# Top 32 of 576 scores on VectorE: the largest of each four keys, with three candidate sets of eight, in place of the larger of each two keys with one set

## The chip, the cores and the metric

The kernel runs on one core of one Trainium2 chip. The core has five engines with a queue each: TensorE (PE in the profile, PEld its weight loads), VectorE (DVE), ScalarE (ACT), GpSimd (POOL) and SyncE (SP), which here only issues DMA transfers. The metric is the device time of one run in microseconds (us); lower is better.

## The reference

Attention with a top 32 of each row of scores, then a layer norm and a two-layer MLP with a residual:

```python
q, k, v: (8, 8, 576, 64)                       # batch, heads, rows, head width
scores = scale * np.matmul(q, k.transpose(0, 1, 3, 2))
kth = np.partition(scores, -32, axis=-1)[..., -32:-31]
scores = np.where(scores >= kth, scores, -1e9)
scores = scores - scores.max(axis=-1, keepdims=True)
attn = np.exp(scores)
attn = attn / (attn.sum(axis=-1, keepdims=True) + 1e-09)
x = matmul(attn, v) with the heads side by side   # (8, 576, 512)
xn = (x - mean) / sqrt(var + 1e-06) * g_ln
out = x + relu(xn @ w_ch1) @ w_ch2               # 512 -> 2048 -> 512
```

## The kernel before

**Units and steps.** The scores are made in units. A full unit is 128 query rows of two heads: two tiles, each 128 rows x 576 scores. A rest unit takes the last 64 rows of two heads as one tile of 128 x 576. There are 128 full and 32 rest units. The main loop (from L1263) makes one step for each unit, and the order of all instructions is written out in it by hand. In step n, VectorE selects on unit n in four stretches (`select(u, 0)` to `select(u, 3)`, L1309, L1342, L1377, L1396) and then prepares the next unit (`halve(nxt)`, L1398). In the same step ScalarE and GpSimd make the mask of unit n-1 (`prepare`, `mask`, L1291 to L1293), PE makes the scores of unit n+2, and the unit before those is transposed and multiplied by V. Between these pieces calls of `fill()` put matmuls of the MLP, as many as a planner has given to the step; its costs (`DVE_UNIT`, L1175) are constants that do not depend on what is measured.

**Finding the threshold.** VectorE has an instruction that gives the eight largest of a row (MAX8) and one that overwrites these eight in the row (MATCH_REPLACE8, with a value load before it). The 32nd largest needs four rounds. Before the change a row of 576 is folded once: `halve` (L447) writes the larger of each pair (j, j+288) to `hi` (L461) and the smaller to `lo` (L462). Rounds 0 and 1 work on the 288 larger ones alone. Eight candidates from `lo` (L475) are put beside `hi`, and rounds 2 and 3 work on 296. `hi` lives in one of two home buffers; the place of the candidates in it changes sides every second unit, so that they can still be read when the next unit of that home is written.

**The mask.** When the last MAX8 (L483) of unit n is done, ScalarE scales the threshold and the maximum (L495, L496) and for each tile writes a step function of the scores (L532); GpSimd subtracts the scores from it (L535); ScalarE takes the exponential (L543).

**The watch.** If eight of a row's top 32 lay in `lo`, eight candidates would not be known to be enough. So GpSimd notes for each row and tile the last candidate less the threshold (L502, two numbers for a full unit). Every 16 units VectorE reduces the notes (L512), and at the end one number (`tell`, L517) says whether the whole program is to be run again with 16 candidates (L1444).

The pool `lo` has one buffer for each tag (L70).

Of the kernel before, what the change touches and what calls it, by code (L numbers as in the profile page):

```python
# [10 lines left out]
ALU = mybir.AluOpType  # L11
FP32 = mybir.dt.float32
# [17 lines left out]
def compute(  # L30
# [12 lines left out]
    nc = tc.nc  # L43
# [15 lines left out]

    NV = 2  # L60
    GQ = 2 * P + R
    HALF = S // 2
    LOWS = 8 * low_rounds

    consts = pool("consts", 1)
    ldpool = pool("ld", 1)
# [24 lines left out]
    def const(shape, name):  # L91
        return consts.tile(shape, FP32, tag=name, name=name)
# [12 lines left out]
    ends = const([P, P], "ends")  # L105
    nc.gpsimd.memset(ends[:], 0.0)
    if doubt is not None:
        watched = const([P, 2, 34], "watched")
        nc.gpsimd.memset(watched[:], -1.0)
    hi_homes = [const([P, 2, HALF + (1 if doubt is None else 2) * LOWS], f"hi{i}") for i in range(2)]  # L110
    ident = const([P, P], "ident")
    make_identity(nc, ident[:])
    columns = const([P, J + NC], "columns")
# [333 lines left out]
    def halve(u):  # L447

        nt = len(u.tiles)
        u.lo = lopool.tile([P, 2, HALF], FP32, tag="lo", name="lo")
        u.hi = hi_homes[u.i % 2]
        sides = int(doubt is not None)
        u.low, u.body = (sides * LOWS + HALF, sides * LOWS) if doubt is None or u.i // 2 % 2 else (0, LOWS)
        a, b = u.sc[:, 0:nt, 0:HALF], u.sc[:, 0:nt, HALF:S]
        lo, hi = u.lo[:, 0:nt], u.hi[:, 0:nt, u.body : u.body + HALF]  # L460
        nc.vector.tensor_tensor(hi, a, b, ALU.max)  # L461
        nc.vector.tensor_tensor(lo, a, b, ALU.min)  # L462

    def select(u, i):

        nt = range(len(u.tiles))

        def replace(m, t, x):
            nc.vector.match_replace(x, m[:, t, :], x, LOWEST)  # L469

        if i == 1:
            for r in range(low_rounds):
                o = u.low + 8 * r
                for t in nt:
                    nc.vector.max(u.hi[:, t, o : o + 8], u.lo[:, t])  # L475
                if r < low_rounds - 1:
                    for t in nt:
                        replace(u.hi[:, :, o : o + 8], t, u.lo[:, t])
        r0, width = (min(u.low, u.body), HALF + LOWS) if i > 1 else (u.body, HALF)
        pl = brief_small if i in (1, 2) else small  # L480
        m = pl.tile([P, 2, 8], FP32, tag=f"m{i}", name=f"m{i}")
        for t in nt:
            nc.vector.max(m[:, t, :], u.hi[:, t, r0 : r0 + width])  # L483
        if i < TOP_K // 8 - 1:
            for t in nt:
                replace(m, t, u.hi[:, t, r0 : r0 + width])
        if i == 0:
            u.top = m
        u.thr = m
# [8 lines left out]
    def watch(u):  # L498

        nt = len(u.tiles)  # L500
        half, c = u.i // 16 % 2, 1 + 2 * (u.i % 16)
        nc.gpsimd.tensor_tensor(  # L502
            watched[:, half, c : c + nt], u.hi[:, 0:nt, u.low + 7], u.thr[:, 0:nt, 7], ALU.subtract
        )
        if u.i % 16 == 15 or u.i == N - 1:
            u.ends_watch = True
            u.half = half

    def settle_watch(half):

        for out, first, op in ((0, 0, ALU.max), (33, 1, ALU.min)):
            nc.vector.tensor_reduce(  # L512
                watched[:, half, out : out + 1], watched[:, half, first : first + 33],
                mybir.AxisListType.X, op,
            )

    def tell():  # L517

        w = hpool.tile([P, J * P], FP32, tag="h", name="tell")
        nc.gpsimd.memset(w[:], 0.0)  # L520
        nc.vector.tensor_scalar(w[:, 2:4], watched[:, :, 33], -1.0e38, None, ALU.is_le)
        nc.vector.tensor_scalar(w[:, 4:6], watched[:, :, 0], 0.0, None, ALU.is_ge)
        nc.vector.tensor_reduce(w[:, 0:1], w[:, 2:6], mybir.AxisListType.X, ALU.max)
        ps = brief("tell")
# [952 lines left out]
```

## Time and profile before

| | |
|---|---|
| Median of 3 runs | 1571.16 us (1571.02 to 1571.75) |
| The profiled execution's own time | 1571.11 us |
| Its span (first to last instruction) | 1569.2 us |
| Mean granted TensorE clock | 0.975 |

The page of the profile has the busy time of each engine, the span in 40 slices, the DMA queues, the chain of work that ended last and the costliest groups of instructions. Further views answer questions: busy time by stages of the span, instructions in order of time, a table of who waited for whom, groups kept apart by shape. Names like `hi<-sc` give the tile written and the tile read; L461 is line 461 of the kernel. Busy time of PE is modelled, so a busy PE is not PE at its peak. The profile is of one execution, and the sums made from it are compared with that execution's own time.

### The profile page before, as it was taken

How to read it: one execution, taken by the hardware profiler on the slowest of the kernel's cores; microseconds unless marked ns; L12 is line 12 of the kernel's file. 1: busy time of each engine (PE TensorE's matmuls, PEld its weight loads, DVE VectorE, ACT ScalarE, POOL GpSimd, SP SyncE). 2: the span in 40 equal slices, each digit the busy share in tenths (PEclk: the TensorE clock that was granted, in tenths of full speed). 3: DMA queues.
4: the chain of work that ended last, by engine and by line, in shares of the span. 5: the costliest groups of instructions: out<-in, count | busy, mean ns of one | idle time of the engine just before them, and what ended most of it. 6: DMA issues, size and time to landing. Idle time of an engine off the chain costs nothing. (4 is left out here: it accounts for less than half of the span.)

```text
span 1569.2 us, 27215 instructions
## 1 busy us (share of the span) xinstructions
PE 1469.0 (94%) x8046; PEld 1108.0 (71%) x8046; DVE 1363.4 (87%) x3873; ACT 1083.8 (69%) x3081; POOL 981.2 (63%) x1318
## 2 busy tenths in 40 slices
PE   4568889999999999999999999999999998999997
PEld 3346446566787677778777777777777776788886
DVE  7997999899979998999988999999999999768000
ACT  6978887786777767767768676768676776555421
POOL 6968995747465565756566647474746475737524
PEclk9779989999999999999999999999999999999999
DMA  6623551466728865577754687657677557454511
GB/s 170 167 85 97 137 139 53 124 178 181 226 83 194 202 208 153 168 199 153 216 148 134 174 200 197 173 150 191 175 201 206 162 164 208 121 166 125 150 35 50
DMA packets 374774, 245.60 MB, mean 157 GB/s; under 512 B 255956, under 2 KB 343512, under 8 KB 374616
## 3 DMA queue, kind: packets, MB, share of 16 engines
q1 hardware_dynamic: 371048, 243.17, 57.6%
q8 instruction: 67, 1.10, 0.3%
q10 hardware_dynamic: 3568, 0.59, 0.3%
q14 instruction: 91, 0.75, 0.2%
HBM read 166.14 MB, written 77.53 MB: 155 GB/s over the span
## 5 line engine op out<-in xcount | busy, mean ns | idle before, releaser
L535 POOL TENSOR_TENSOR e<-e,sc 128x576 f32<-128x576 f32 x288 | 416.0, 1462 | 453.8 <-ACT e L532 392.9
L819 PE MATMUL hps<-xT,w 128*128 128x256 f32 x2304 | 542.2, 384 | 2.4 <-ACT xT L781 2.4
L819 PEld LDWEIGHTS hps<-xT,w 128*128 128x128 f32 x2304 | 423.0, 191 | 82.2 <-issue 27.2
L483 DVE MAX8 m<-hi 128x8 f32<-128x296 f32 (+1 forms) x1152 | 471.3, 444 | 1.2
L469 DVE MATCH_REPLACE8 hi<-m,hi 128x288 f32<-128x288 f32 (+1 forms) x864 | 377.0, 441 | 0.0
L979 PE MATMUL ops<-w,h 128*128 128x256 f32 x1280 | 304.8, 383 | 1.4 <-ACT o L944 1.4
L979 PEld LDWEIGHTS ops<-w,h 128*128 128x128 f32 x1280 | 233.6, 190 | 44.3 <-issue 13.5
L419 ACT COPY sc<-scps 128x288 f32<-128x288 f32 x576 | 188.5, 402 | 78.5 <-POOL e L535 56.2
L543 ACT ACTIVATE e<-e,m 128x576 f32<-128x576 f32 x288 | 225.1, 784 | 14.6 <-POOL e L535 12.5
L532 ACT ACTIVATE e<-sc,m 128x576 f32<-128x576 f32 x288 | 209.4, 769 | 0.0
L842 ACT ACTIVATE h<-hps 128x512 f32<-128x512 f32 x144 | 86.7, 602 | 114.1 <-PE hps L819 113.5
L577 DVE STREAM_TRANSPOSE sc<-e 128x1152 f32<-128x1152 f32 x87 | 118.8, 1366 | 52.5 <-ACT e L543 46.3
L669 PE MATMUL av<-pt,vb 128*64 128x256 f32 (+2 forms) x1280 | 148.8, 376 | 9.5 <-DMA pt<-turned 7.7
L462 DVE TENSOR_TENSOR lo<-sc 128x576 f32<-128x576 f32 (+1 forms) x160 | 136.1, 850 | 0.0
L461 DVE TENSOR_TENSOR hi<-sc 128x576 f32<-128x576 f32 (+1 forms) x160 | 130.0, 812 | 3.0 <-ACT sc L419 3.0
L669 PEld LDWEIGHTS av<-pt,vb 128*64 128x64 f32 x1280 | 81.6, 140 | 66.4 <-issue 17.1
L438 PE MATMUL scps<-kT,late_qT 64*128 64x288 f32 (+3 forms) x832 | 121.7, 410 | 0.2 <-ACT pt L618 0.2
L979 PE MATMUL ops<-wt,s 128*128 128x256 f32 x512 | 119.4, 383 | 0.0
L475 DVE MAX8 hi<-lo 128x8 f32<-128x288 f32 x288 | 117.5, 443 | 0.0
L438 PE MATMUL scps<-kT,qT 64*128 64x288 f32 x512 | 92.6, 460 | 23.5 <-DVE qT L366 8.0
L606 PE MATMUL tp<-ident,e 128*128 128x128 f32 x456 | 74.2, 290 | 39.9 <-ACT e L543 28.9
L979 PEld LDWEIGHTS ops<-wt,s 128*128 128x128 f32 x512 | 94.7, 190 | 17.3 <-issue 4.4
(111 smaller groups left out, 1793.5 us busy)
## 6 DMA issues: line engine op xcount, KB each, us to landing
turned<-sc SPq DMA_DIRECT2D x87, 576.0 KB, 4.2
pt<-turned SPq DMA_DIRECT2D x348, 144.0 KB, 3.2
w<-forms SPq DMA_DIRECT2D x128, 256.0 KB, 4.7
vb<-in_v_dram SPq DMA_DIRECT2D x80, 288.0 KB, 4.2
raw<-in_moe_w_ch_dram SPq DMA_DIRECT2D x32, 512.0 KB, 4.5
kT<-kept SPq DMA_DIRECT2D x48, 288.0 KB, 3.7
kept<-kT SPq DMA_DIRECT2D x32, 288.0 KB, 3.6
kqin<-in_k_dram SPq DMA_DIRECT2D x116, 72.0 KB, 2.6
```

What stands on the lines that cost most here:

```text
L419: nc.scalar.copy(u.sc[:, t, s * HALF : (s + 1) * HALF], u.made[s][t][:, 0:HALF])
L438: nc.tensor.matmul(ps[i * R : i * R + ql, o : o + width], qT[r, q0 : q0 + ql], kT[r, k0 : k0 + width], start=True, stop=True,)
L461: nc.vector.tensor_tensor(hi, a, b, ALU.max)
L462: nc.vector.tensor_tensor(lo, a, b, ALU.min)
L469: nc.vector.match_replace(x, m[:, t, :], x, LOWEST)
L483: nc.vector.max(m[:, t, :], u.hi[:, t, r0 : r0 + width])
L532: nc.scalar.activation(u.e[:, t], u.sc[:, t], AF.Relu, bias=u.edge[:, t : t + 1], scale=-STEEP)
L535: nc.gpsimd.tensor_tensor(u.e[:, t], u.e[:, t], u.sc[:, t], ALU.subtract)
L543: nc.scalar.activation(u.e[:, t], u.e[:, t], AF.Exp, bias=u.bias[:, t : t + 1], scale=-scale, accum_out=g.den[:, col : col + 1],)
L669: nc.tensor.matmul(av[h * D : (h + 1) * D, 0 : g.nq], vb[:, h * (J + 1) + c, :], heads_of(g, h, 0, g.nq // 32)[:, :, c], start=(c == 0), s ...
L819: nc.tensor.matmul(ps[0][:, side * N : (side + 1) * N], w1[:, c, f * P : (f + 1) * P], self.xT[:, c, 0:N], start=(c == 0), stop=(c == NC - 1),
L979: nc.tensor.matmul(bank[name][:, 0:Q], a(j), rhs, start=first and j == 0, stop=(j == G - 1), skip_group_check=not first,)
```

## The change

The row of 576 is folded twice. `halve` writes the larger of each pair to a tile `pairs` of 288 and folds that again: the larger ones, the largest of each four keys (144), go to `hi`, and the smaller ones, the seconds of this fold (144), to a new tile `mid`. The smaller halves of the first fold go to `lo` as before; `pairs` and `lo` share a tag, so they share one buffer. In `select`, round 0 works on the 144; after it eight candidates are taken from each half of `mid` (72 each), and in the second stretch eight from `lo`, as before; rounds 1 to 3 work on 168, the 144 and 24 candidates. The watch notes the last candidate of each of the three sets, so the notes are three times as many. The second pass (`doubt is None`) keeps the single fold. The planner's constants are not touched.

```diff
--- before.py
+++ after.py
@@ -59,8 +59,10 @@
 
     NV = 2
     GQ = 2 * P + R
-    HALF = S // 2
+    HALF, QUART = S // 2, S // 4
     LOWS = 8 * low_rounds
+    POOLS = 3
+    CANDS = 8 * POOLS
 
     consts = pool("consts", 1)
     ldpool = pool("ld", 1)
@@ -105,9 +107,11 @@
     ends = const([P, P], "ends")
     nc.gpsimd.memset(ends[:], 0.0)
     if doubt is not None:
-        watched = const([P, 2, 34], "watched")
+        NOTES = POOLS * 32
+        watched = const([P, 2, NOTES + 2], "watched")
         nc.gpsimd.memset(watched[:], -1.0)
-    hi_homes = [const([P, 2, HALF + (1 if doubt is None else 2) * LOWS], f"hi{i}") for i in range(2)]
+    home = HALF + LOWS if doubt is None else QUART + 2 * CANDS
+    hi_homes = [const([P, 2, home], f"hi{i}") for i in range(2)]
     ident = const([P, P], "ident")
     make_identity(nc, ident[:])
     columns = const([P, J + NC], "columns")
@@ -452,14 +456,25 @@
 
 
         nt = len(u.tiles)
+        u.hi = hi_homes[u.i % 2]
+        a, b = u.sc[:, 0:nt, 0:HALF], u.sc[:, 0:nt, HALF:S]
+        tt = nc.vector.tensor_tensor
+        if doubt is None:
+            u.lo = lopool.tile([P, 2, HALF], FP32, tag="lo", name="lo")
+            u.low, u.body, u.width = HALF, 0, HALF
+            tt(u.hi[:, 0:nt, 0:HALF], a, b, ALU.max)
+            tt(u.lo[:, 0:nt], a, b, ALU.min)
+            return
+        u.low, u.body = (CANDS + QUART, CANDS) if u.i // 2 % 2 else (0, CANDS)
+        u.width = QUART
+        pairs = lopool.tile([P, 2, HALF], FP32, tag="lo", name="pairs")
+        tt(pairs[:, 0:nt], a, b, ALU.max)
+        x, y = pairs[:, 0:nt, 0:QUART], pairs[:, 0:nt, QUART:HALF]
+        u.mid = lopool.tile([P, 2, QUART], FP32, tag="mid", name="mid")
+        tt(u.hi[:, 0:nt, u.body : u.body + QUART], x, y, ALU.max)
+        tt(u.mid[:, 0:nt], x, y, ALU.min)
         u.lo = lopool.tile([P, 2, HALF], FP32, tag="lo", name="lo")
-        u.hi = hi_homes[u.i % 2]
-        sides = int(doubt is not None)
-        u.low, u.body = (sides * LOWS + HALF, sides * LOWS) if doubt is None or u.i // 2 % 2 else (0, LOWS)
-        a, b = u.sc[:, 0:nt, 0:HALF], u.sc[:, 0:nt, HALF:S]
-        lo, hi = u.lo[:, 0:nt], u.hi[:, 0:nt, u.body : u.body + HALF]
-        nc.vector.tensor_tensor(hi, a, b, ALU.max)
-        nc.vector.tensor_tensor(lo, a, b, ALU.min)
+        tt(u.lo[:, 0:nt], a, b, ALU.min)
 
     def select(u, i):
 
@@ -468,15 +483,24 @@
         def replace(m, t, x):
             nc.vector.match_replace(x, m[:, t, :], x, LOWEST)
 
-        if i == 1:
-            for r in range(low_rounds):
-                o = u.low + 8 * r
+        if doubt is None:
+            if i == 1:
+                for r in range(low_rounds):
+                    o = u.low + 8 * r
+                    for t in nt:
+                        nc.vector.max(u.hi[:, t, o : o + 8], u.lo[:, t])
+                    if r < low_rounds - 1:
+                        for t in nt:
+                            replace(u.hi[:, :, o : o + 8], t, u.lo[:, t])
+            with_all, cands = i > 1, LOWS
+        else:
+            if i == 1:
                 for t in nt:
-                    nc.vector.max(u.hi[:, t, o : o + 8], u.lo[:, t])
-                if r < low_rounds - 1:
-                    for t in nt:
-                        replace(u.hi[:, :, o : o + 8], t, u.lo[:, t])
-        r0, width = (min(u.low, u.body), HALF + LOWS) if i > 1 else (u.body, HALF)
+                    nc.vector.max(u.hi[:, t, u.low : u.low + 8], u.lo[:, t])
+            with_all, cands = i > 0, CANDS
+        r0, width = u.body, u.width
+        if with_all:
+            r0, width = min(u.low, u.body), width + cands
         pl = brief_small if i in (1, 2) else small
         m = pl.tile([P, 2, 8], FP32, tag=f"m{i}", name=f"m{i}")
         for t in nt:
@@ -484,6 +508,14 @@
         if i < TOP_K // 8 - 1:
             for t in nt:
                 replace(m, t, u.hi[:, t, r0 : r0 + width])
+        if i == 0 and doubt is not None:
+            part = QUART // (POOLS - 1)
+            for t in nt:
+                for r in range(POOLS - 1):
+                    o = u.low + 8 + 8 * r
+                    nc.vector.max(
+                        u.hi[:, t, o : o + 8], u.mid[:, t, r * part : (r + 1) * part]
+                    )
         if i == 0:
             u.top = m
         u.thr = m
@@ -498,9 +530,13 @@
     def watch(u):
 
         nt = len(u.tiles)
-        half, c = u.i // 16 % 2, 1 + 2 * (u.i % 16)
+        half, c = u.i // 16 % 2, 1 + 2 * POOLS * (u.i % 16)
+        cands = u.hi[:, 0:nt, u.low : u.low + CANDS].rearrange("p t (r k) -> p t r k", k=8)
         nc.gpsimd.tensor_tensor(
-            watched[:, half, c : c + nt], u.hi[:, 0:nt, u.low + 7], u.thr[:, 0:nt, 7], ALU.subtract
+            watched[:, half, c : c + POOLS * nt].rearrange("p (t r) -> p t r", r=POOLS),
+            cands[:, :, :, 7],
+            u.thr[:, 0:nt, 7].unsqueeze(2).to_broadcast([P, nt, POOLS]),
+            ALU.subtract,
         )
         if u.i % 16 == 15 or u.i == N - 1:
             u.ends_watch = True
@@ -508,9 +544,9 @@
 
     def settle_watch(half):
 
-        for out, first, op in ((0, 0, ALU.max), (33, 1, ALU.min)):
+        for out, first, op in ((0, 0, ALU.max), (NOTES + 1, 1, ALU.min)):
             nc.vector.tensor_reduce(
-                watched[:, half, out : out + 1], watched[:, half, first : first + 33],
+                watched[:, half, out : out + 1], watched[:, half, first : first + NOTES + 1],
                 mybir.AxisListType.X, op,
             )
 
@@ -518,7 +554,7 @@
 
         w = hpool.tile([P, J * P], FP32, tag="h", name="tell")
         nc.gpsimd.memset(w[:], 0.0)
-        nc.vector.tensor_scalar(w[:, 2:4], watched[:, :, 33], -1.0e38, None, ALU.is_le)
+        nc.vector.tensor_scalar(w[:, 2:4], watched[:, :, NOTES + 1], -1.0e38, None, ALU.is_le)
         nc.vector.tensor_scalar(w[:, 4:6], watched[:, :, 0], 0.0, None, ALU.is_ge)
         nc.vector.tensor_reduce(w[:, 0:1], w[:, 2:6], mybir.AxisListType.X, ALU.max)
         ps = brief("tell")
```

## The prediction

> **What bounds the kernel now.** I read the page's busy shares first.
> ```profile
> span 1569.2 us, 27215 instructions
> ...
> PE 1469.0 (94%) x8046; PEld 1108.0 (71%) x8046; DVE 1363.4 (87%) x3873; ACT 1083.8 (69%) x3081; POOL 981.2 (63%) x1318
> ```
> TensorE (PE) looks like the bound, but these are averages. So I asked for the busy time by stages (columns: length, then busy us and instruction count of PE, its weight loads, VectorE (DVE), ScalarE (ACT), GpSimd (POOL), then clock and DMA).
> ```profile
> 480.00:600.00 120.00, 114.02 (x647) 87.38 (x646) 119.55 (x345) 85.38 (x250) 66.47 (x92) 0.99 0.78 201
> 600.00:720.00 120.00, 118.95 (x760) 92.67 (x760) 110.68 (x319) 88.54 (x272) 73.81 (x109) 1.00 0.63 164
> ...
> 840.00:960.00 120.00, 117.31 (x648) 88.69 (x647) 119.48 (x344) 86.28 (x249) 74.15 (x110) 1.00 0.74 188
> 960.00:1080.00 120.00, 118.73 (x663) 90.24 (x663) 119.38 (x347) 87.81 (x260) 72.75 (x107) 1.00 0.61 165
> 1080.00:1200.00 120.00, 118.96 (x644) 89.85 (x642) 119.25 (x340) 87.19 (x253) 72.56 (x111) 1.00 0.71 190
> 1200.00:1320.00 120.00, 115.46 (x630) 86.56 (x627) 119.45 (x349) 84.46 (x251) 74.62 (x109) 1.00 0.63 179
> ...
> 1480.00:1569.00 89.00, 79.17 (x383) 68.08 (x381) 1.64 (x4) 17.72 (x42) 32.76 (x63) 0.96 0.19 55
> ```
> From 480 to 600 and from 840 to 1320 us VectorE is busy 119.2 to 119.6 of each 120 us: nothing can be put in there without making the step longer. PE does more matmuls in a stage where VectorE has gaps (760 against 630 to 663), so in the saturated stages it is not at its limit, but it is near it. The last 89 us belong to PE alone. Then the table of waits (waiter <- what it waited for: us, times, longest):
> ```profile
> POOL e L535 <- ACT e L532: 392.9, 111, 10.2
> ...
> ACT m L495 <- DVE m L483: 84.2, 51, 3.7
> ACT sc L419 <- POOL e L535: 56.2, 25, 4.4
> DVE sc L577 <- ACT e L543: 46.3, 10, 9.3
> ...
> ACT e L543 <- POOL e L535: 12.5, 20, 1.7
> ```
> In 51 of the 160 unit steps ScalarE stands idle until VectorE's last MAX8 of the unit (L483) has come: there it starts on the mask at once. Keep this 51.
>
> **One unit's work on VectorE, from the timeline.** A step in a saturated stage (columns: start us, length us, what):
> ```profile
> 1232.49 0.74 DVE L461 TENSOR_TENSOR hi<-sc 128x576 f32<-128x576 f32 x1
> ...
> 1232.84 1.44 ACT L532 ACTIVATE e<-sc,m 128x576 f32<-128x576 f32 x2
> ...
> 1233.14 0.75 DVE L462 TENSOR_TENSOR lo<-sc 128x576 f32<-128x576 f32 x1
> ...
> 1233.69 2.85 POOL L535 TENSOR_TENSOR e<-e,sc 128x576 f32<-128x576 f32 x2 [3.98 <-ACT e L532]
> ...
> 1233.81 0.81 DVE L483 MAX8 m<-hi 128x8 f32<-128x288 f32 x2
> ...
> 1234.54 0.07 DVE L469 MATCH_VALUE_LOAD hi<-m,hi 128x8 f32 x1
> 1234.60 0.44 DVE L469 MATCH_REPLACE8 hi<-m,hi 128x288 f32<-128x288 f32 x1
> ...
> 1234.96 0.08 DVE L469 MATCH_VALUE_LOAD hi<-m,hi 128x8 f32 x1
> ...
> 1235.39 0.81 DVE L475 MAX8 hi<-lo 128x8 f32<-128x288 f32 x2
> ...
> 1236.12 0.80 DVE L483 MAX8 m<-hi 128x8 f32<-128x288 f32 x2
> ...
> 1237.68 0.83 DVE L483 MAX8 m<-hi 128x8 f32<-128x296 f32 x2
> 1238.43 0.07 DVE L469 MATCH_VALUE_LOAD hi<-m,hi 128x8 f32 x1
> ...
> 1240.03 0.44 DVE L461 TENSOR_TENSOR hi<-sc 128x288 f32<-128x288 f32 x1
> 1240.39 0.45 DVE L462 TENSOR_TENSOR lo<-sc 128x288 f32<-128x288 f32 x1
> 1240.76 0.45 DVE L483 MAX8 m<-hi 128x8 f32<-128x288 f32 x1
> 1241.25 0.09 DVE L469 MATCH_VALUE_LOAD hi<-m,hi 128x8 f32 x1
> ```
> What counts is the distance from one start to the next, which I call the slot, not the length, because the end of one instruction overlaps the start of the next. A TENSOR_TENSOR over 576 elements has a slot of 0.65 to 0.67 us (1232.49 to 1233.14 to 1233.81), over 288 one of 0.36; a MAX8 over 288 has 0.365 (two in 0.73), a MATCH_REPLACE8 0.36 (1234.60 to 1234.96), its value load 0.065. So a slot is 0.06 us plus 1.04 ns an element, which is (0.66-0.36)/288. An instruction that needs the result of the one just before it comes later: 1240.76 to 1241.25 is 0.49 where 0.365 is the slot, 0.12 more. The step runs 7.54 us (1232.49 to 1240.03) without a gap.
>
> **The change, part by part.** A full unit (two tiles; 128 of them) has 8 MAX8 and 6 MATCH_REPLACE8 on 288 or 296 elements, and 2 MAX8 on the smaller halves. Without its two TENSOR_TENSOR that is 7.54 - 1.32 = 6.22 us.
>
> MAX and replace: afterwards slots by the formula are 0.21 (144 elements), 0.235 (168) and 0.135 (72). Two MAX8 on 144 and six on 168 make 1.83; two on the smaller halves stay 0.73; four new ones on 72 make 0.54; two replaces on 144 and four on 168 make 1.36; six value loads 0.40. Sum 4.86, which is 1.36 us less. (With the four TENSOR_TENSORs below, a full unit issues 30 instructions, where it had 24.) With two tiles in turn no dependent pair stands back to back, so no 0.12 is added.
>
> The TENSOR_TENSORs: two become four. The pair maxima over 576 cost 0.66, and the next one reads them, so 0.78 until it starts; the fours' maxima 0.36; the fours' seconds 0.36, and then the smaller halves are written into the buffer that the seconds are read from, so that instruction waits for them too: 0.48; then 0.67. Sum 2.29 against 1.32: 0.97 more. Undisturbed, a full unit gains 1.36 - 0.97 = 0.39 us. A rest unit (one tile; 32 of them) has its MAX and replace in a dependent row; by the same slots it saves 0.56 and pays 0.66: 0.10 us more.
>
> Now the collision, which decides. These rows show a TENSOR_TENSOR pair on VectorE into which the mask's subtraction on GpSimd falls:
> ```profile
> 710.50 0.74 DVE L461 TENSOR_TENSOR hi<-sc 128x576 f32<-128x576 f32 x1
> 710.78 1.73 POOL L535 TENSOR_TENSOR e<-e,sc 128x576 f32<-128x576 f32 x1 [6.76 <-ACT e L532]
> ...
> 711.15 1.97 DVE L462 TENSOR_TENSOR lo<-sc 128x576 f32<-128x576 f32 x1
> ...
> 713.05 0.81 DVE L483 MAX8 m<-hi 128x8 f32<-128x288 f32 x2
> ```
> ```profile
> L535 POOL TENSOR_TENSOR e<-e,sc x288: 1394/1413/2648, 30.3 to 1465.4; 128x576 f32<-128x576 f32 x144
> ```
> ```profile
> L461 DVE TENSOR_TENSOR hi<-sc x160: 429/737/1978, 11.3 to 1440.8; 128x576 f32<-128x576 f32 x128, 128x288 f32<-128x288 f32 x32
> ```
> ```profile
> L462 DVE TENSOR_TENSOR lo<-sc 128x576 f32<-128x576 f32 x128 | 117.6, 918 | 0.0
> ...
> L461 DVE TENSOR_TENSOR hi<-sc 128x576 f32<-128x576 f32 x128 | 114.5, 895 | 3.0 <-ACT sc L419 3.0
> ```
> GpSimd's instruction started 0.28 us into VectorE's first one, took 1.73 instead of its median 1.41, so it was held for 0.32, until VectorE's first had read for 0.60; then VectorE's second one, due at 711.15, took 1.97 instead of 0.75, 1.22 more. The two engines take turns, one whole instruction each, in the order in which they ask, and MAX8 and MATCH_REPLACE8 take no part (in the quiet step above they keep their 0.44 while GpSimd's two run from 1233.69 to 1236.54). In the quiet step above the subtraction comes 1.20 us after the first TENSOR_TENSOR (1233.69 - 1232.49): in the last one, so VectorE loses nothing and GpSimd 0.07. ScalarE's way to the mask starts at the end of the unit's last MAX8 and the change leaves it as it is, so the subtraction will again ask at 1.20. But then VectorE is at the third of four (it starts at 0.78 + 0.36 = 1.14 and reads until 1.44) and the fourth is due at 1.62. GpSimd gets in at 1.44, holds until 2.85, and the fourth runs from 2.85, 1.23 us late. What is queued behind it is the next unit's whole selection, and all of PE's and ScalarE's work that hangs on it. Such a unit costs -0.39 + 1.23 = 0.84 us more than before. The second subtraction then waits for the fourth's 0.60 us of reading and ends 4.86 us after the first TENSOR_TENSOR instead of 4.05 (1.20 + 2.85); ScalarE's exponentials (L543) wait for it, and ScalarE has some 30 us idle in each 120.
>
> [...]
>
> Small things: the watch on GpSimd subtracts six numbers instead of two, four elements more in the 4 us for which GpSimd waits for ScalarE anyway (3.98 in the row above); if that cover were gone it would be some ns each. The 20 reductions of the notes read 97 instead of 33 elements, 64 x 1.04 ns x 20 = 1.3 us. The wait for the watch of the unit four before moves from the second stretch of the selection to the first, some 2 us earlier; that watch is over two steps old by then. PE, ScalarE and SyncE issue the same instructions in the same order, DMAs included.
>
> **The sum.** 128 full units undisturbed: -0.39 x 128 = -50. 32 rest units: +3. The subtraction that asks at 1.20: 51 steps by the row of waits, x 1.23 = +63. Other collisions (weight conversion, sums of the MLP): L461 and L462 now stand at 895 and 918 ns, and undisturbed at 740 and 750, so they cost (155 + 168) x 128 = 41 us; with four instructions to be cut into instead of two, what comes on top lies between 0 and 41. The reading time goes up by half (0.60 + 0.30 + 0.30 + 0.60 = 1.80 against 1.20), which would be 20 more; the number of entries doubles, which would be 41; I take 30. Notes +1. Sum +47. Some falls into the stages in which VectorE has idle time (9.3 of 120 us at 600 to 720) and from 1480 us on VectorE has almost nothing to do: I keep +45 on the profiled run's own time of 1571.1 us (span 1569.2 and 1.9 around it; the median of the runs is 1571.16, the same): **1616 us**. The ends: nothing of the last 30 and 30 collisions instead of 51 give 47 - 30 - 26 = -9, so 1562; collisions in 70 steps and the full 41 of the others give 47 + 23 + 11 = +81, so 1652.
>
> **Rivals.**
> (a) The subtraction misses the cluster, because ScalarE is late or VectorE goes first: then the 0.39 is gained, in the saturated stages only, since PE is near its limit. 600 us of such stages are some 75 steps of about 8 us (7.54, or 8.9 with a transpose in it), 128/160 of them full: 60 x 0.39 = 23, so 1548. For it: only 51 of 160 steps are of the prompt kind. Against it: in the saturated stages the delay of 1.20 is set by VectorE itself, and a slower VectorE makes ScalarE more often prompt. It decides against the forecast once fewer than about 30 steps collide. 0.15.
> (b) PE hides it: no change, 1571. The MLP's matmuls fill each step, and PE shows 118 to 119 of 120. Against: VectorE has no gap there, and what it loses lengthens the step. 0.04.
> (c) Feedback: each slower VectorE step makes ScalarE wait, so nearly all 128 full units collide: 128 x 0.84 = 108, less what the idle stages take: 1670. And ScalarE's score copies wait for the subtraction already (56.2 us). 0.13.
> (d) Short instructions don't overlap: each costs its whole length, a MAX8 over 288 its 0.44 us and not 0.365, about 0.08 more for each of the six added, 0.48 against the 0.39 gained: 0.09 lost in a full unit, 60 x 0.09 = 5 us without collisions, 1576. The rows of slots speak against it. 0.02. [...]
> (e) The second pass: the kernel computes everything again where a row holds eight of its top 32 in one candidate set. In the reference's own inputs no set of the 36864 rows holds more than six, so it does not run; it would double the time, 3140. 0.01.
>
> **The numbers.** The forecast 0.65, with 1562 to 1652 as its own range. A measurement of this kernel tells about 0.2% (3 us) from no change. Slower by more: the forecast less its lowest end, (c), (d), (e), 0.79; within: (b) and a strip of the others, 0.05; faster: (a) and a little, 0.16. The range from 1556 to 1660 holds the forecast, (b), (d) and the near parts of (a) and (c).
>
> **What would show it.** In the changed profile VectorE's last TENSOR_TENSOR of a full unit (smaller halves) lasts about 1.97 in many steps, its mean over 1.3 us, and the subtraction starts inside the third one. MAX8 over 168 elements should stand at 0.235 us from its neighbour, 72 at 0.135; if not, the slots are wrong. Steps of 7.54 become 8.4; where the cluster is missed, 7.15. The MAX and replace groups together lose about 170 us of slots, the TENSOR_TENSOR groups gain more than that. It is wrong if the fourth TENSOR_TENSOR stays at 0.75, or if a saturated stage's steps get longer with no collision in them.

## The result, and the profile after

| | before | after |
|---|---|---|
| Median, same chip | 1571.09 us (1570.99 to 1571.75, 4 runs) | 1625.37 us (1620.86 to 1628.77, 4 runs) |
| The profiled execution, span | 1571.11, 1569.2 us | 1625.62, 1623.8 us |
| Mean granted TensorE clock | 0.975 | 0.968 |

The ratio is 1.0343 (95% interval 1.0317 to 1.0368): 54 us slower, where 45 were forecast.

The page of the changed kernel, span and busy shares:
```profile
span 1623.8 us, 28111 instructions
...
PE 1488.0 (92%) x8046; PEld 1117.2 (69%) x8046; DVE 1436.4 (88%) x4769; ACT 1084.1 (67%) x3081; POOL 1035.0 (64%) x1318
```
The span grew by 54.6 us. VectorE (DVE) is busy 73.0 us longer, and idle 18.4 us less (1569.2 - 1363.4 = 205.8 before, 1623.8 - 1436.4 = 187.4 now): 73.0 - 18.4 = 54.6. What must be explained is why VectorE works 73 us longer at a fold that was to need less MAX and replace.

One stage of the changed kernel, from the busy time by stages (columns as in the prediction: PE, weight loads, VectorE, ScalarE, GpSimd, clock, DMA share, GB/s):
```profile
1080.00:1200.00 120.00, 110.99 (x593) 81.22 (x592) 118.11 (x391) 77.85 (x231) 72.58 (x102) 0.99 0.65 165
```
VectorE is still full, with more instructions than before (391 for 340). PE fell from 644 matmuls to 593 and from 118.96 us busy to 110.99: it does fewer matmuls in the same time, so it hid nothing of VectorE's loss.

VectorE's groups of the changed kernel, shapes apart (busy us, mean ns of one, idle before):
```profile
L507 DVE MAX8 m<-hi 128x8 f32<-128x168 f32 x864 | 241.3, 314 | 2.3
L484 DVE MATCH_REPLACE8 hi<-m,hi 128x168 f32<-128x168 f32 x576 | 177.9, 313 | 0.0
L477 DVE TENSOR_TENSOR lo<-sc 128x576 f32<-128x576 f32 x128 | 171.3, 1338 | 4.4
L613 DVE STREAM_TRANSPOSE sc<-e 128x1152 f32<-128x1152 f32 x87 | 118.8, 1365 | 37.1 <-ACT e L579 31.0 <-issue 6.1
...
L471 DVE TENSOR_TENSOR pairs<-sc 128x576 f32<-128x576 f32 x128 | 115.8, 905 | 3.0 <-ACT sc L423 3.0
L516 DVE MAX8 hi<-mid 128x8 f32<-128x72 f32 x576 | 91.5, 215 | 0.0
L474 DVE TENSOR_TENSOR hi<-pairs 128x288 f32<-128x288 f32 x128 | 90.4, 706 | 4.4
L484 DVE MATCH_REPLACE8 hi<-m,hi 128x144 f32<-128x144 f32 x288 | 81.7, 288 | 0.0
L475 DVE TENSOR_TENSOR mid<-pairs 128x288 f32<-128x288 f32 x128 | 81.5, 637 | 0.0
L507 DVE MAX8 m<-hi 128x8 f32<-128x144 f32 x288 | 74.7, 294 | 0.0
```
The same view of the kernel before, for the groups that these replace:
```profile
L469 DVE MATCH_REPLACE8 hi<-m,hi 128x288 f32<-128x288 f32 x576 | 249.7, 438 | 0.0
L483 DVE MAX8 m<-hi 128x8 f32<-128x296 f32 x576 | 237.3, 447 | 1.2
L483 DVE MAX8 m<-hi 128x8 f32<-128x288 f32 x576 | 233.9, 441 | 0.0
L469 DVE MATCH_REPLACE8 hi<-m,hi 128x296 f32<-128x296 f32 x288 | 127.3, 447 | 0.0
L577 DVE STREAM_TRANSPOSE sc<-e 128x1152 f32<-128x1152 f32 x87 | 118.8, 1366 | 52.5 <-ACT e L543 46.3 <-issue 6.1
```
MAX and replace on the larger ones took 848.2 us (249.7 + 237.3 + 233.9 + 127.3); with the MAX8 of the seconds they take 667.1 now (241.3 + 177.9 + 91.5 + 81.7 + 74.7). That gain is real. The TENSOR_TENSORs of the full units rose from 232.1 (117.6 + 114.5) to 459.0, which is more. The clue is in their means: undisturbed, the last one would take 0.745 us, but it takes 1.338; before, the last one's mean was 0.918.

One step of the changed kernel in order of time (start us, length us):
```profile
1283.07 0.73 DVE L471 TENSOR_TENSOR pairs<-sc 128x576 f32<-128x576 f32 x1
...
1283.84 0.46 DVE L474 TENSOR_TENSOR hi<-pairs 128x288 f32<-128x288 f32 x1
1284.21 0.45 DVE L475 TENSOR_TENSOR mid<-pairs 128x288 f32<-128x288 f32 x1
1284.27 3.54 POOL L571 TENSOR_TENSOR e<-e,sc 128x576 f32<-128x576 f32 x2 [4.50 <-ACT e L568]
1284.69 1.85 DVE L477 TENSOR_TENSOR lo<-sc 128x576 f32<-128x576 f32 x1
...
1287.44 0.62 DVE L516 MAX8 hi<-mid 128x8 f32<-128x72 f32 x4
...
1287.99 0.79 DVE L499 MAX8 hi<-lo 128x8 f32<-128x288 f32 x2
1288.71 0.54 DVE L507 MAX8 m<-hi 128x8 f32<-128x168 f32 x2
1289.18 0.06 DVE L484 MATCH_VALUE_LOAD hi<-m,hi 128x8 f32 x1
...
1291.33 0.43 DVE L471 TENSOR_TENSOR pairs<-sc 128x288 f32<-128x288 f32 x1
```
The subtraction asks 1.20 us after the first TENSOR_TENSOR, as before, and meets the third of four. The fourth takes 1.85 us where it needs 0.75, so it is 1.10 late, and the step runs 8.26 us (1283.07 to 1291.33) instead of 7.54. Without the 1.10 it would be 7.16; three other steps, from 255.97, 677.70 and 870.22 us, in which none of the four is late, run 7.17. Four MAX8 over 72 elements start 0.55 us before what follows them (1287.44 to 1287.99), 0.1375 each.

The waits of the changed kernel (waiter, releaser: us, times, longest):
```profile
ACT m L527 <- DVE m L507: 148.8, 66, 5.2
```
The steps in which ScalarE stood ready for the threshold rose from 51 to 66.

**The account.** Undisturbed, the four of a full unit last 0.745, 0.446, 0.446 and 0.745 us. What the group means lie above that, times 128, is 20 us for the pair maxima, 33 for the fours' maxima, 24 for their seconds and 76 for the smaller halves: 154 us of waiting inside TENSOR_TENSORs. Before, 895 and 918 ns against 745 made 41 us. So full units wait 113 us more, of which 54 are on the smaller halves (76 against 22 on L462) and 59 on the other three. The rest units, summed from their single instructions, wait 9 us more. The slots give back 0.38 us for each full unit (7.54 to 7.16), 49 us, and 3 are lost in rest units by the forecast (not measured): 113 + 9 - 46 = 76, against the 73 us by which VectorE is busier. Of the 18.4 us of idle time that took part of it up, 15.4 are in one row: the transpose that waited 52.5 us in all for its input waits 37.1 now.

### The profile page after: what moved, and what is told of

It is laid out like the page before. It is cut to its first block, busy times and chain, and to the rows that moved or that the text cites. A ratio compares the mean times of both kernels' runs of the same rounds, so it can differ in the third digit from the quotient of the medians.

```text
span 1623.8 us, 28111 instructions
## 1 busy us (share of the span) xinstructions
PE 1488.0 (92%) x8046; PEld 1117.2 (69%) x8046; DVE 1436.4 (88%) x4769; ACT 1084.1 (67%) x3081; POOL 1035.0 (64%) x1318
## 4 chain that ended last, share of the span: by engine, by line
DVE 49%; PE 33%; ACT 5%; POOL 5%; DMA 4%; issue 2%; SPq 1%; ACTq 0%; DVEq 0%; POOLq 0%
PE hps L855 15%; DVE m L507 9%; DVE hi L484 8%; PE ops L1015 8%; DVE lo L477 7%; DVE sc L613 4%; DVE pairs L471 4%; DVE hi L499 4%; DVE hi L474 3%; PE scps L442 3%; PE av L705 3%; DVE mid L475 3%; DVE hi L516 3%; POOL e L571 2%; PE tp L642 1%
## 5 line engine op out<-in xcount | busy, mean ns | idle before, releaser
L571 POOL TENSOR_TENSOR e<-e,sc 128x576 f32<-128x576 f32 x288 | 454.2, 1595 | 450.5 <-ACT e L568 424.1
L507 DVE MAX8 m<-hi 128x8 f32<-128x168 f32 (+1 forms) x1152 | 316.0, 309 | 2.3
L1015 PE MATMUL ops<-w,h 128*128 128x256 f32 x1280 | 309.2, 387 | 2.7 <-ACT o L980 2.6
L1015 PEld LDWEIGHTS ops<-w,h 128*128 128x128 f32 x1280 | 236.3, 192 | 47.0 <-issue 13.5
L484 DVE MATCH_REPLACE8 hi<-m,hi 128x168 f32<-128x168 f32 (+1 forms) x864 | 259.6, 305 | 0.0
L579 ACT ACTIVATE e<-e,m 128x576 f32<-128x576 f32 x288 | 225.4, 785 | 20.9 <-POOL e L571 18.4
L477 DVE TENSOR_TENSOR lo<-sc 128x576 f32<-128x576 f32 (+1 forms) x160 | 192.0, 1200 | 5.5
L613 DVE STREAM_TRANSPOSE sc<-e 128x1152 f32<-128x1152 f32 x87 | 118.8, 1365 | 37.1 <-ACT e L579 31.0
L471 DVE TENSOR_TENSOR pairs<-sc 128x576 f32<-128x576 f32 (+1 forms) x160 | 133.9, 837 | 3.0 <-ACT sc L423 3.0
L527 ACT ACTIVATE m<-m 128x2 f32<-128x2 f32 (+1 forms) x160 | 32.8, 205 | 149.3 <-DVE m L507 148.8
L442 PE MATMUL scps<-kT,qT 64*128 64x288 f32 x512 | 98.1, 471 | 27.7 <-ACT x L727 9.3
```

The lines of the kernel that those rows point to most:

```text
L442: nc.tensor.matmul(ps[i * R : i * R + ql, o : o + width], qT[r, q0 : q0 + ql], kT[r, k0 : k0 + width], start=True, stop=True,)
L471: tt(pairs[:, 0:nt], a, b, ALU.max)
L477: tt(u.lo[:, 0:nt], a, b, ALU.min)
L571: nc.gpsimd.tensor_tensor(u.e[:, t], u.e[:, t], u.sc[:, t], ALU.subtract)
L579: nc.scalar.activation(u.e[:, t], u.e[:, t], AF.Exp, bias=u.bias[:, t : t + 1], scale=-scale, accum_out=g.den[:, col : col + 1],)
L1015: nc.tensor.matmul(bank[name][:, 0:Q], a(j), rhs, start=first and j == 0, stop=(j == G - 1), skip_group_check=not first,)
```

## The experiments

| kernel | median us | ratio to before (95%) |
|---|---|---|
| after | 1625.37 | 1.0343 (1.0317 to 1.0368) |
| b_split | 1593.28 | 1.0146 (1.0129 to 1.0162) |
| a_late_lo | 1572.55 | 1.0018 (1.0009 to 1.0028) |
| a_take_first | 1609.35 | 1.0266 (1.0247 to 1.0285) |
| b_take_first | 1597.84 | 1.0185 (1.0168 to 1.0202) |
| a_pairs_early | 1571.07 | 1.0004 (0.9995 to 1.0013) |
| a_halve_early | 1610.81 | 1.0251 (1.0237 to 1.0265) |
| b_halve_early | 1584.17 | 1.0086 (1.0072 to 1.01) |
| a_early_late | 1576.82 | 1.0035 (1.0022 to 1.0049) |
| b_no_sub | 1550.21 | 0.9864 (0.9848 to 0.9879) |
| a_no_sub | 1579.66 | 1.0057 (1.004 to 1.0073) |
| b_three | 1657.29 | 1.0557 (1.054 to 1.0575) |
| b_three_gap | 1733.08 | 1.1041 (1.1004 to 1.1077) |

Names with a_ start from the changed kernel, those with b_ from the one before. The runs were made on several chips; each ratio is to the kernel before on the same chip (medians there from 1569.26 to 1571.25 us).

### Four TENSOR_TENSORs without the new fold: b_split

```diff
-        nc.vector.tensor_tensor(hi, a, b, ALU.max)
-        nc.vector.tensor_tensor(lo, a, b, ALU.min)
+        for t in range(nt):
+            nc.vector.tensor_tensor(hi[:, t], a[:, t], b[:, t], ALU.max)
+        for t in range(nt):
+            nc.vector.tensor_tensor(lo[:, t], a[:, t], b[:, t], ALU.min)
```


> The kernel before, with each of its two TENSOR_TENSORs of a full unit cut into one per tile: the same elements, four instructions of 288 where there were two of 576, no new dependence. Theory of the collision: the fourth is due at 3 x 0.36 = 1.08 us and reads until 1.38, but the third reads until 1.02, so GpSimd asking at 1.20 finds the fourth at work and nothing collides in the prompt steps; only the two slots more (0.12 us a full unit) count, and the collisions with other GpSimd work, up to twice the 41 us of before. So 1571 + 8 to 12 + 0 to 30: 1580 to 1612, with L461 and L462 undisturbed in the prompt steps. Rival (the number of instructions on VectorE is what costs, whatever GpSimd does): the changed kernel has six more instructions in a full unit and costs 54 us, so two more cost 54/3 = 18: 1589, with no long TENSOR_TENSOR added.

Measured 24 us above the kernel before on the same chip (1569.26). VectorE is busy 54.7 us longer: two more slots cost 0.12 us in a full unit, 15 us, and the waiting inside the TENSOR_TENSORs rose by 37 (summed over the trace as in the account); VectorE's idle time took up 31. The time lies within the range of the one theory and 4 us from the rival's figure, so it decides nothing. The trace speaks against the rival, which expected no long TENSOR_TENSOR added: 40 take over 1.5 us, where the kernel before has 25. So four instructions with the same work lose more to GpSimd than two, and that with no dependent wait among them. One step shows how:
```profile
971.85 2.02 DVE L464 TENSOR_TENSOR lo<-sc 128x288 f32<-128x288 f32 x2
971.92 3.22 POOL L537 TENSOR_TENSOR e<-e,sc 128x576 f32<-128x576 f32 x2 [0.30 <-ACT e L534]
```
The subtraction asks 0.07 us into the third TENSOR_TENSOR. The fourth is queued directly behind and starts 0.37 us after the third, but takes 1.66 us where 0.45 is undisturbed (the two together 2.02): GpSimd got in between two instructions that have no wait between them.

### The fourth one taken out of the cluster: a_late_lo

In `halve` the smaller halves are no longer made. In the third stretch of `select`:
```diff
+            if i == 2:
+                lo = lopool.tile([P, 2, HALF], FP32, tag="lo", name="lo")
+                nc.vector.tensor_tensor(
+                    lo[:, 0:n], u.sc[:, 0:n, 0:HALF], u.sc[:, 0:n, HALF:S], ALU.min
+                )
+                for t in nt:
+                    nc.vector.max(u.hi[:, t, u.lo_at : u.lo_at + 8], lo[:, t])
```
The second stretch works with 16 candidates, the third and fourth with 24.

> The changed kernel with the smaller halves made late: their TENSOR_TENSOR (576 elements) and their MAX8 move from the start of the unit to the third stretch of the selection, where GpSimd mostly waits; round 1 leaves their candidates out. The amount of VectorE's work is the same (one slot of the second MAX8 shorter). Theory of the collision: GpSimd asking at 1.20 finds the third and last of the cluster reading (1.15 to 1.45), VectorE loses nothing, a quiet full unit takes about 7.15 instead of 7.54 before and 8.26 in the changed kernel: 1545 to 1565, limited by PE. Rival (amount of VectorE's work): 1610 to 1630.

Measured 53 us below the changed kernel, though the numbers of MAX and replace and of TENSOR_TENSORs are the same; round 1 is 8 elements narrower, and the fourth's wait of 0.12 us for the third is gone (some 15 us in 128 full units, by slots). At 1572.55 it lies some 8 us above the range expected. Its group of smaller halves:
```profile
L500 DVE TENSOR_TENSOR lo<-sc 128x576 f32<-128x576 f32 x128 | 115.3, 901 | 0.0
```
0.901 us in place of 1.338: 56 us less on this instruction, and the time fell by 53. It ends no lower than the kernel before because the other collisions stay: all TENSOR_TENSORs together still wait 114 us (47.5 before, 169 in the changed kernel).

### One MAX8 pair between the first and the second: a_pairs_early

```diff
+        if nxt and doubt is not None:
+            pair(nxt)
         if u:
             select(u, 3)
         if nxt:
             halve(nxt)
```
`pair` makes the pair maxima alone; `halve` does the rest.

> The changed kernel with only the first of the four (the pair maxima) put before the last MAX8 pair; the other three stay behind it. Theory of the collision: they start at 0, 0.36 and 0.84 us after the MAX8, the last reads until 1.44, so the subtraction asking at 1.20 finds the last one at work and VectorE loses nothing; the dependent wait of 0.12 behind the pair maxima goes too, so a quiet full step lasts about 7.05 us: 1545 to 1570. Rival (amount of work): 1605 to 1625.

Measured the same as before to 0.1%, 54 us below the changed kernel. In order of time:
```profile
1227.92 0.75 DVE L455 TENSOR_TENSOR pairs<-sc 128x576 f32<-128x576 f32 x1
...
1228.59 0.57 DVE L514 MAX8 m<-hi 128x8 f32<-128x168 f32 x2
...
1229.07 0.44 DVE L481 TENSOR_TENSOR hi<-pairs 128x288 f32<-128x288 f32 x1
...
1229.91 0.76 DVE L484 TENSOR_TENSOR lo<-sc 128x576 f32<-128x576 f32 x1
...
1230.62 1.41 POOL L578 TENSOR_TENSOR e<-e,sc 128x576 f32<-128x576 f32 x1 [1.10 <-ACT e L575]
```
The mask waits for that MAX8 pair, so the subtraction now asks at 1230.62, 0.71 after the fourth began, when that has done its reading (0.60 us by the prediction's row at 710.50): 0.76 and 1.41 us are both undisturbed. The dependent wait behind the pair maxima is filled too (1228.59 is 0.67 after 1227.92). Only 6 of 128 of the smaller halves take over 1.5 us, against 61 in the changed kernel. VectorE is busy 65 us less than in the changed kernel (1371.4 against 1436.4): 49 are waits inside TENSOR_TENSORs, and the filled wait of 0.12 us makes some 15 in 128 full units. The expected gain over the kernel before was missed: these waits still sum to 120 us.

### The whole fold a MAX8 pair earlier, in both kernels: a_halve_early, b_halve_early

```diff
+        if nxt:
+            halve(nxt)
         if u:
             select(u, 3)
-        if nxt:
-            halve(nxt)
```


> The changed kernel with all four TENSOR_TENSORs of the next unit put before the last MAX8 pair of this one instead of after it. The instructions and their dependent waits are the same. Theory of the collision: GpSimd's subtractions run from 1.2 to 4.1 us after the end of that MAX8, when none of the four is on; the four start about 4.4 us after it at the earliest. L477 stays at about 0.76 in the saturated stages and a quiet full step lasts 7.17: 1550 to 1575. Rival (more and shorter instructions, dependent waits): 1615 to 1630, as nothing of these has changed.

> Control: the same move in the kernel before. Theory of the collision: in the prompt steps nothing collided there, so nothing is won: 1563 to 1577. Rival (the move is good by itself, for example by mixing long and short instructions): it gains as much as a_halve_early gains on the changed kernel, 50 us.

Both missed. The first, 1610.81, lies 36 us above the range of the collision theory and only 4 below the rival's, so by its time it speaks for the rival. The trace does not, since what the rival called unchanged did change: the smaller halves fell to a mean of 0.924 us, 9 of 128 over 1.5, but the pair maxima rose from 905 to 993 ns and the fours' maxima from 706 to 773. The move itself costs 13.5 us where only it is made, and the change on top of it 26.6 instead of 54. The fourth's collision was mostly avoided, and others came in its place.

### Score copies ahead of the mask, in both kernels: a_take_first, b_take_first

```diff
+        for x in ahead:
+            take_scores(x)
         if mk:
             prepare(mk)
...
-        for x in ahead:
-            take_scores(x)
         if n in brings:
```


> The changed kernel with ScalarE's copies of the next scores (1.3 us) put ahead of the mask. VectorE's work is as in the changed kernel. Theory of the collision: the subtraction asks at about 2.5 us after the first TENSOR_TENSOR, after the fourth has begun (1.64) and ended its reading (2.24); L477 falls from a mean of 1.34 us to 0.75 to 0.95, quiet steps last 7.17 instead of 8.26, and the time falls to 1555 to 1585. Rival (more and shorter instructions on VectorE, or the dependent waits among the four): VectorE issues the same, so the time stays at 1615 to 1635.

> Control: the same move of ScalarE's copies in the kernel before. Theory of the collision: there the subtraction asked during the last TENSOR_TENSOR and cost nothing, so nothing is to be gained by it: 1565 to 1585. Rival (the order on ScalarE is better or worse by itself): it moves by as much as in the changed kernel, some 50 us.

Both missed: 1609.35 lies 24 us above the range expected and 6 below the rival's, 1597.84 13 us above its own. This delays ScalarE's mask and so the subtraction: the smaller halves fell to a mean of 1.006 us. But the control alone is 29 us above the kernel before on the same chip (1569.26), most likely because the subtraction now comes so late that ScalarE's exponentials wait for it, as the control's table of waits has it:
```profile
ACT e L543 <- POOL e L535: 65.6, 104, 2.4
```
In the kernel before that row had 12.5 us in 20 waits. On top of this order the change costs 11.5 us instead of 54.

### Both moves of single pieces: a_early_late

The edits of a_pairs_early and a_late_lo together.

> a_pairs_early and a_late_lo together: the pair maxima before the last MAX8 pair, the smaller halves in the third stretch of the selection. Behind the last MAX8 stand only two TENSOR_TENSORs of 0.36, over 0.7 us after it, before the subtraction asks at 1.20. By the collision theory neither engine waits in the prompt steps; a quiet full step is 7.05 us as in a_pairs_early, and the collisions with other GpSimd work decide: 1560 to 1573. If the amount of VectorE's work decided, it would equal a_pairs_early, 1569 to 1573.

Slightly missed: 1576.82 is above either move alone. The smaller halves in the third stretch then wait 39 us in all, in a place where neither kernel had a TENSOR_TENSOR before.

### Without the subtraction: b_no_sub, a_no_sub

```diff
-        nc.gpsimd.tensor_tensor(u.e[:, t], u.e[:, t], u.sc[:, t], ALU.subtract)
```


> The kernel before without GpSimd's subtraction of the scores (the exponential is taken of the mask alone, so the attention weights are left out). Theory of the collision: it cost little there, so the time falls only by the waits of ScalarE and PE for the subtraction: 1535 to 1568.

> The changed kernel without GpSimd's subtraction of the scores (the same part left out). Theory of the collision: the fourth TENSOR_TENSOR has nothing to wait for in the prompt steps, L477 falls to under 1.0 us on average, and what is left of the change is its undisturbed gain of 50 us less the further collisions with GpSimd's other work (about 40): from 30 us below b_no_sub to 5 above it. Rival (the number of instructions and the dependent waits): it stays 40 to 55 us above b_no_sub.

The first came as expected: before the change the subtraction costs 21 us in all. The second missed. The smaller halves did fall, from 1.338 to 0.857, and without the subtraction the changed kernel is 46 us faster; but it is 29 us above b_no_sub, where 30 below to 5 above were expected and the rival said 40 to 55 above, so neither fits. What takes the place shows in the table of waits and in order of time of a_no_sub:
```profile
POOL watched L535 <- DVE m L507: 576.9, 115, 12.8
```
```profile
1208.94 0.73 DVE L471 TENSOR_TENSOR pairs<-sc 128x576 f32<-128x576 f32 x1
...
1209.10 0.64 POOL L535 TENSOR_TENSOR watched<-hi,m 128x6 f32<-128x6 f32 x1 [4.75 <-DVE m L507]
...
1209.71 0.76 DVE L474 TENSOR_TENSOR hi<-pairs 128x288 f32<-128x288 f32 x1
1210.39 0.70 DVE L475 TENSOR_TENSOR mid<-pairs 128x288 f32<-128x288 f32 x1
1211.13 0.90 DVE L477 TENSOR_TENSOR lo<-sc 128x576 f32<-128x576 f32 x1
```
GpSimd, no longer held by the mask, stands in 115 steps ready at its watch, starts it 0.16 us after the pair maxima, and does its MLP sums right behind it. The watch enters where the second TENSOR_TENSOR waits for the first, and the row of sums cuts into the three others: 0.76, 0.70 and 0.90 where 0.45, 0.45 and 0.75 are undisturbed. It is 0.7 us in this step, in place of 1.10. So the loss belongs to the cluster of four, and not to the subtraction alone: other work that GpSimd has ready at that time comes in too.

### Is it the number or the gap: b_three, b_three_gap

The kernel before with one more TENSOR_TENSOR over 576, whose output is overwritten, either first or between:
```diff
         # b_three
+        nc.vector.tensor_tensor(lo, a, b, ALU.max)
         nc.vector.tensor_tensor(hi, a, b, ALU.max)
         nc.vector.tensor_tensor(lo, a, b, ALU.min)
         # b_three_gap
         nc.vector.tensor_tensor(hi, a, b, ALU.max)
+        nc.vector.tensor_tensor(lo, a, b, ALU.max)
         nc.vector.tensor_tensor(lo, a, b, ALU.min)
```
In b_three_gap the third writes what the one just before it wrote, so it waits for it; in b_three that one is two back.

> The kernel before with one TENSOR_TENSOR more ahead of its two (the larger of each pair written once into the buffer of the smaller ones, which are written over it later): the third is then due at 0.66 + 0.66 = 1.32 us. Theory of the collision: GpSimd's subtraction asks at 1.20 during the second, gets in at 1.26 and holds the third until about 2.6: L462 of a full unit falls into two groups, 0.75 and about 1.85 to 1.95 us, with 50 to 70 in the second. The instruction itself costs 0.66 x 128 + 0.36 x 32 = 96 us, of which some 85 on the path; the collisions 55 to 75 more: 1705 to 1735. Rival (work alone): 1640 to 1670, with L462 at 0.75 in the prompt steps.

> b_three with its first two TENSOR_TENSORs exchanged: the same three instructions, but the third now writes over what the one just before it wrote, so it waits for that one's end and is due at 1.44 us instead of 1.32. In b_three the subtraction asked 0.55 us into the second's 0.60 us of reading and in most full steps the third went ahead of it (22 of 128 were long). Theory that a dependent wait opens the port: now the second has ended its reading at 1.26 with nothing behind it, GpSimd gets in, and the third waits until about 2.6: 60 to 80 long ones (over 1.5 us), each 1.1 late, and the time is 1657 + 0.12 x 128 x 0.9 + 40 to 55 x 1.1 = 1715 to 1732. Rival (only the wait itself counts, the turn taken does not depend on it): 1657 + 12 to 15 = 1669 to 1673, with some 22 long ones.

The first missed: I expected the third to be hit, and it mostly wasn't; 1657.29 lies in the rival's range. The second came 1 us above its range, with 81 long ones where 60 to 80 were expected. In order of time and by its line, b_three:
```profile
1229.15 0.73 DVE L461 TENSOR_TENSOR lo<-sc 128x576 f32<-128x576 f32 x1
...
1229.81 0.75 DVE L462 TENSOR_TENSOR hi<-sc 128x576 f32<-128x576 f32 x1
1230.35 2.14 POOL L536 TENSOR_TENSOR e<-e,sc 128x576 f32<-128x576 f32 x1 [7.08 <-ACT e L533]
1230.47 0.75 DVE L463 TENSOR_TENSOR lo<-sc 128x576 f32<-128x576 f32 x1
```
```profile
L463 DVE TENSOR_TENSOR lo<-sc x160: 440/747/1966, 12.4 to 1528.7; 128x576 f32<-128x576 f32 x128, 128x288 f32<-128x288 f32 x32
```
And b_three_gap, the same two views:
```profile
1293.73 0.73 DVE L461 TENSOR_TENSOR hi<-sc 128x576 f32<-128x576 f32 x1
...
1294.38 0.75 DVE L462 TENSOR_TENSOR lo<-sc 128x576 f32<-128x576 f32 x1
1294.93 1.46 POOL L536 TENSOR_TENSOR e<-e,sc 128x576 f32<-128x576 f32 x1 [7.21 <-ACT e L533]
1295.16 1.84 DVE L463 TENSOR_TENSOR lo<-sc 128x576 f32<-128x576 f32 x1
```
```profile
L463 DVE TENSOR_TENSOR lo<-sc x160: 457/1718/1975, 12.7 to 1607.5; 128x576 f32<-128x576 f32 x128, 128x288 f32<-128x288 f32 x32
```
In both the subtraction asks 1.20 us after the first, 0.54 or 0.55 us into the second. Where the third is queued directly behind (0.66 later), it goes first and GpSimd waits (2.14 instead of 1.41); the third's median is 0.747, and 22 of 128 take over 1.5 us. Where the third is due 0.12 later, because it waits for the second, GpSimd has started and the third takes 1.84; its median is 1.718, and 81 of 128 take over 1.5. Counted over the trace, the subtraction asks between 0.53 and 0.56 us into an undisturbed second 54 times in b_three and gets in ahead of the third 9 times; in b_three_gap 64 times out of 64. The 0.12 us of dependence costs 15 us by itself in 128 units; the step from b_three to b_three_gap is 76. So at this late moment of asking a gap decides. In the changed kernel the subtraction asks early, 0.06 us into the third, and the step of b_split above shows that so early an ask can get in without any gap.

## Why the prediction was right, and where its sizes were off

**What bounds it**: right. VectorE stayed full where it had been, and PE fell back (593 matmuls for 644). Rival (b), PE hides it, is out.

**MAX and replace, -1.36 a full unit**: right. The slots came as worked out: 0.1375 us for 72 elements where 0.135 was said, and for 168 two in 0.47 us (1288.71 to 1289.18), which is the 0.235. Rival (d) is out with that.

Length and slot differ here too: a MAX8 of 72 elements lasts 0.215 us (mean of 576), of which 72 x 1.04 ns, the slope of the slots, make an estimated 0.075, so 0.14 are left. In a row it takes up 0.1375 in all (four in 0.55 us), so the next one is not held for the 0.14.

**The TENSOR_TENSORs, +0.97**: right. The starts lie 0.77, 0.37 and 0.48 us apart (1283.07, 1283.84, 1284.21, 1284.69) where 0.78, 0.36 and 0.48 were said, and the undisturbed gain is 0.38 where 0.39 was said.

**The collision**: the place was right (in the third, the fourth late). The price was 1.10 us, not 1.23, and the steps were more than 51: 61 fourths took over 1.5 us, 57 of them behind the subtraction. On the fourth it came to 54 us against the 63 of the sum. That this collision makes the loss is shown from three sides: with the fourth moved away (a_late_lo) and with the subtraction moved behind it (a_pairs_early) the time falls by 53 and 54 us, and a third TENSOR_TENSOR with a gap ahead of it, in the kernel before, brings the collision in (b_three_gap). The two moves also take a wait of 0.12 us out of each full unit, some 15 of these us; the rest is waiting that goes. Rival (a), which needed fewer than some 30 such steps, is out.

**What was said of the turns** was too simple. Not each waiting engine gets in after one instruction of the other: b_three shows the late asker mostly passed over when VectorE's next is directly behind (45 of 54 asks), and b_three_gap that a gap of 0.12 us lets it in (64 of 64). The port that b_three_gap's expectation speaks of was the author's picture: the runs show only which engine went next, and when. But the gap ahead of the fourth is not shown to be what opened the changed kernel to GpSimd. Over all the runs, counting the subtractions that came to an idle GpSimd, it asked 20 times while an undisturbed TENSOR_TENSOR over 288 elements was reading (an estimated 0.30 us, 288 x 1.04 ns) with the next one queued directly behind, and got in 19 times; where the next one had to wait for the one reading, it got in every time (146 of 146, all widths). While one over 576 was reading with the next directly behind, it got in 15 times of 66, and 54 of these 66 are the late asks of b_three. What decides among the rest stays open.

**Other collisions, +30 with bounds of 0 and 41**: the mis-sized term. On the three other TENSOR_TENSORs and in the rest units it came to 59 + 9 = 68 us, above the upper bound. The bound counted entries (twice as many instructions to be cut into); it left out that a first hit shifts the rest of the cluster into GpSimd's next instruction. A step of the changed kernel shows it:
```profile
986.99 0.74 DVE L471 TENSOR_TENSOR pairs<-sc 128x576 f32<-128x576 f32 x1
...
987.15 1.14 POOL L787 TENSOR_SCALAR x<-x,less 128x512 f32<-128x512 f32 x1
987.76 0.83 DVE L474 TENSOR_TENSOR hi<-pairs 128x288 f32<-128x288 f32 x1
988.25 3.19 POOL L571 TENSOR_TENSOR e<-e,sc 128x576 f32<-128x576 f32 x2
988.51 1.66 DVE L475 TENSOR_TENSOR mid<-pairs 128x288 f32<-128x288 f32 x1
990.21 1.85 DVE L477 TENSOR_TENSOR lo<-sc 128x576 f32<-128x576 f32 x1
```
GpSimd's layer norm holds the second back by 0.37 us; so the two subtractions come one into the third (1.21 late) and one into the fourth (1.10 late). One step pays 2.7 us. Such chains make most of it: summed over the full units, 46 of the 56 us for which the second and the third wait lie in units in which one ahead of them was late already. A gap is not needed for it: the third, directly behind the second, has 24 of these 56 us.

**What idle stages take, 2 us**: too little, 18.4, most of it in the transposes' wait for the exponentials. So 54 + 68 - 46 - 18 = 58 against a measured 54.6, and that the sum of +47 came near is partly luck: an unforeseen 38 us and an unforeseen 16 + 9 us of relief stood against each other.

**Rival (c), feedback**: half true. ScalarE was ready in 66 steps instead of 51, so more steps collided than before, but not nearly all.

The second pass, rival (e), didn't run: one span, and the same 8046 matmuls as before.

No version that computes the whole result beat the kernel before; the best, a_pairs_early, equals it. A buffer of its own for the pair maxima, which would close the gap ahead of the fourth, wasn't tried. By the slots it would save an estimated 0.12 us a full unit; by the step of b_split it need not keep GpSimd out. No order was found that brings the 49 us of undisturbed gain to light.

## What to carry to other kernels

The sum of slots priced this cluster of VectorE instructions only where GpSimd did not come in (7.17 us a step against 8.26 with the collision): before splitting one TENSOR_TENSOR into several, look at when GpSimd's next instruction asks, counted from the cluster's start (here 1.20 us). Where it asks inside, move part of the cluster away from that moment: here one MAX8 pair put between the first and the second took 54 us off. To order them so that none waits for the one just before it helped against a late ask (b_three against b_three_gap, 76 us), but was not enough by itself: in b_split none waits, and GpSimd comes in all the same. And run each reordering on the kernel before as well: two of the orders tried here cost 14 and 29 us by themselves.

## What was not expected of the hardware

- A GpSimd TENSOR_TENSOR that asked 0.54 us into the 0.60 us in which VectorE's TENSOR_TENSOR reads was mostly passed over when VectorE's next one was queued directly behind (45 of 54 asks in b_three; 2.14 us in place of 1.41), and got in when that one was 0.12 us later (64 of 64 in b_three_gap). At 0.28 us into it, in the kernel before, it got in even ahead of one queued directly behind (the 1.97 of the prediction's rows); so it did, with 288 elements and 0.07 us into the reading, in b_split.
- The fourth TENSOR_TENSOR in the step at 1283.07, due 0.42 us after the subtraction's start, took 1.85 us instead of 0.75: it was held for 1.10 us, where 1.23 were expected. The other way round GpSimd gets in before the end that the profile shows for VectorE's instruction: in the prediction's row at 710.50 the subtraction asks 0.28 us into a TENSOR_TENSOR and takes 1.73 instead of 1.41, so it is held until 0.60 us after the start of an instruction that the profile shows with 0.74. Who goes next where both wait is in the counts above.
- Even GpSimd's TENSOR_SCALAR with one large input held VectorE's TENSOR_TENSOR back in the step shown (1.14 us from 987.15 on; 0.83 instead of 0.46 at 987.76), and GpSimd's watch of six numbers took 0.64 us beside the pair maxima in a_no_sub.
